# Attention outputs in the two column halves of the array, v rows with their neighbours, and an earlier begin of the first GEMM

## The chip, the cores and the metric

The kernel runs on one core of a Trainium2 chip. The metric is the device time of one execution in microseconds (us), lower is better. The runs of the kernel before took 255.43 us in the median of three (255.09 to 257.05). Differences of less than about 1% cannot be told from none.

The engines are TensorE (PE: matmuls into the accumulation memory, PSUM, and beside them weight loads, PEld), VectorE (DVE), ScalarE (ACT), GpSimd (POOL) and SyncE (SP). GpSimd and SyncE also issue DMAs. Each engine works through its own instructions in order and waits on semaphores of the others.

## What is computed

For 4 batches, 8 heads, 768 positions and head size 64, attention with a local window and block summaries, then a feed-forward layer with a hard-swish:

```python
k_sum = k.reshape(B, H, nb, 32, D).max(axis=3)       # nb = 24 blocks of 32 keys
v_sum = v.reshape(B, H, nb, 32, D).mean(axis=3)
scores_l = q k^T / sqrt(D), kept where |i - j| < 16
scores_s = q k_sum^T / sqrt(D) + log(32)
a = softmax([scores_l, scores_s])
x = a @ [v, v_sum]                                    # heads side by side: 3072 x 512
h = x @ w_in                                          # 512 x 2048
out = (h * clip(h + 3, 0, 6) / 6) @ w_out             # 2048 x 512
```

## The kernel before, in words

A query block has 64 positions. The keys that it can see are its own 64, the 16 before and the 16 after, and the 24 block summaries: 120 of 128 rows of a contraction. So for each head and query block one matmul makes the scores, transposed (keys on the rows, 64 queries on the columns), and one makes the values. The heads are handled in four pairs (head p with head p + 4); a batch has two halves of 384 positions, six query blocks each. One half of a batch is one tile of the feed-forward layer, so there are eight tiles of 384 rows.

The steps, by their helper and line in the kernel before:

- `load` (L220), `load_vf` (L237), `edges_v` (L262), `load_v` (L273), `load_vrows` (L280), `load_w_in`, `load_w_out`: loads, all issued on GpSimd's queue. At most eight of them are under way: the ninth is issued when the first has landed.
- `Tk`, `Tq` (L495, L537): transposes of k and q by TensorE, 96 rows at a time, head j of a pair into column half j; ScalarE and VectorE copy them out. `Tk` also makes the block maxima and copies each block's neighbours beside it (`side`, two copies).
- `Sc` (L566): scores `sp`, 12 matmuls per pair and half, head j in row half j of the array; exp on ScalarE (L588), the mask on VectorE (L591).
- `AV` (L602): values `nd`. For each head and query block a matmul of the 128 key rows with 128 weight columns, of which one half are v and the other half fill. For batches 0 and 1 the fill is zero: both heads accumulate into one PSUM tile `num` (L618), and two more matmuls with ones give the sums of the exponentials in `den` (L623). For batches 2 and 3 (`DEN_IN_VALUES`, L29) the fill is ones: one matmul gives values and denominator together, `num` and `den` hold one head each with the halves swapped, and the logarithm and the final multiply are done in two instructions of 64 rows (L631, L632, L644, L645) in place of one of 128 (L634, L647). L635 turns the logarithm into a reciprocal.
- `F1` (L662): GEMM 1 of a tile, 16 column blocks of four matmuls (one per pair) into `hp` (L672), a ReLU on ScalarE (L677) and a min-and-multiply on VectorE (L680) into `g`.
- `F2` (L688): GEMM 2, 48 matmuls of 512 columns per tile (L700), in groups of three; each finished block of 128 rows is copied by ScalarE (L705) and stored by SyncE (L707).

The key rows of v stand in two buffers, `va[0]` for even batches and `va[1]` for odd ones: rows 0 to 63 own keys, 64 to 87 block sums, 96 to 111 the next 16 keys, 112 to 127 the previous 16. For batches 1 to 3 one DMA per four heads loads the own rows (L275) and two per four heads the edges (L266); v is loaded once more as rows of 32 keys (L283), GpSimd adds them to block sums (`vsum`, L288, five additions per four heads), and SyncE spreads the sums to all query blocks, one put per pair and four heads (L298). SyncE's puts and its output stores stand in one queue, in order. Batch 0 does not wait for this: v is loaded in float32 (`vf`), cast by three engines (L254), and its sums come from TensorE (`sum_v`, L725) and are copied to the query blocks (L743).

The order of the instructions on each engine comes from a planner (`class Plan`, L33). Each operation is added with an engine, an estimated cost, keys that it reads and writes, the buffers that it takes and a place; the planner simulates the engines and emits, engine by engine, the ready operation with the lowest place. A place is a number on a scale where each GEMM column block is one step: negative places are the start-up, 0 to 15 is GEMM 1 of tile 0, and so on. `attention(b, s)` (L803) puts the attention of batch b into the GEMM slots before tile 2b. In idle time at the start the planner puts `fill` matmuls on TensorE (L429).

## Time and profile before

| | |
|---|---|
| median of three runs | 255.43 us |
| the profiled execution's own time | 252.96 us |
| its span, first to last instruction | 251.3 us |
| mean granted TensorE clock | 0.986 |
| GEMM 1: 512 matmuls of 384 columns | 94.3 us busy |
| GEMM 2: 384 matmuls of 512 columns (358 in the records) | 90.0 us busy |
| values: 384 matmuls of 64 columns, and 32 with ones of 384 | 17.1 and 8.2 us busy |
| moved by DMA | 28.33 MB in 53851 packets |

How to read it: a busy time of matmuls counts each from its start to the modelled end, so neighbours overlap; the pace is better read from the starts in the timeline. Rows of groups give line, engine, operation, output and input, shape and count, then the busy time and the mean of one in ns, then the idle time of the engine before them and what ended it. In the timeline a row is a run of equal instructions: start, time covered, engine, line. DMA rows end with the median time from issue to landing.

### The profile page before, as it was taken

The numbers are of one execution on the slowest core, as the hardware profiler recorded it, in microseconds if no ns is written. First come the engines' busy times: TensorE is split into PE (matmuls) and PEld (weight loads), VectorE is DVE, ScalarE is ACT, GpSimd is POOL, SyncE is SP. The second block draws the span as 40 slices with busy tenths as digits, with TensorE's granted clock in tenths as the row PEclk, the third lists the DMA queues.
The fourth block names the chain that finished last, engine by engine and source line by source line (L and its number), as shares of the span: only waits on it lengthen the run. The fifth ranks groups of instructions, "written<-read, shape, count | busy, mean of one in ns | idle before, by whom it ended". The sixth has DMA issues, their size and how long they took to land.

```text
span 251.3 us, 5636 instructions
## 1 busy us (share of the span) xinstructions
PE 230.8 (92%) x2247; PEld 127.8 (51%) x2273; DVE 157.8 (63%) x309; ACT 163.5 (65%) x321; POOL 97.8 (39%) x134
## 2 busy tenths in 40 slices
PE   5899699999993997999989999999999999999993
PEld 1385456555552455665545555555455455555541
DVE  5568888658871237999687798468674735444400
ACT  2346679765650558986789885798786956555420
POOL 8985962757997704769990010000000000000000
PEclk9999999999997799999999999999999999999999
DMA  5999999999989999419992101100111021011112
GB/s 64 214 202 177 207 203 206 213 254 173 187 168 186 199 215 205 144 26 194 191 122 68 42 3 44 42 34 11 44 42 42 3 83 43 3 43 43 42 44 83
DMA packets 53851, 28.33 MB, mean 113 GB/s; under 512 B 39808, under 2 KB 49280, under 8 KB 53248
## 3 DMA queue, kind: packets, MB, share of 16 engines
q0 software_dynamic: 42384, 20.68, 62.5%
q1 hardware_dynamic: 11440, 7.28, 10.3%
q8 instruction: 18, 0.29, 0.5%
q14 instruction: 9, 0.07, 0.1%
HBM read 35.06 MB, written 6.29 MB: 165 GB/s over the span
## 4 chain that ended last, share of the span: by engine, by line
PE 79%; ACT 6%; DVE 5%; DMA 5%; issue 2%; POOL 1%; SPq 0%; ACTq 0%; POOLq 0%
PE hp L672 31%; PE op L700 30%; PE nd L618 4%; DMA va<-vs 3%; PE sums L729 3%; PE sp L584 3%; PE tpq L549 2%; PE fill L429 2%; PE tpk L504 2%; DMA stg<-in_k_dram 2%; PE nd L623 2%; DVE at L591 1%; ACT at L588 1%; ACT lg L635 1%; DVE g L680 1%
## 5 line engine op out<-in xcount | busy, mean ns | idle before, releaser
L677 ACT ACTIVATE r<-hp,half_c 128x384 f32<-128x384 f32 x128 | 71.9, 580 | 35.7 <-PE hp L672 32.1
L672 PE MATMUL hp<-x,win 128*128 128x384 bf16 x512 | 94.3, 326 | 0.7 <-DVE g L680 0.5
L700 PE MATMUL op<-wout,g 128*128 128x512 bf16 x358 | 90.0, 385 | 2.6 <-issue 1.8
L680 DVE SCALAR_TENSOR_TENSOR g<-r,hp 128x384 bf16<-128x384 f32 x128 | 67.6, 550 | 30.9 <-ACT r L677 28.2
L672 PEld LDWEIGHTS <-win 128*128 128x128 bf16 x512 | 48.0, 98 | 35.6 <-issue 2.0
L700 PEld LDWEIGHTS <-g 128*128 128x128 bf16 x384 | 36.0, 99 | 38.1 <-issue 1.9
L588 ACT ACTIVATE at<-sp 128x384 bf16<-128x384 f32 x64 | 27.7, 486 | 6.0 <-PE sp L584 5.9
L295 POOL TENSOR_TENSOR vr<-vr 96x1024 f32<-96x1024 f32 (+3 forms) x24 | 30.0, 1252 | 1.4
L591 DVE TENSOR_TENSOR at<-at,mask 128x768 bf16<-128x768 bf16 x32 | 21.9, 683 | 9.0 <-ACT at L588 8.8
L618 PE MATMUL nd<-at,va 128*128 128x64 bf16 x384 | 17.1, 194 | 6.7 <-DMA va<-vs 3.7
L705 ACT COPY ot<-op 128x512 f32<-128x512 f32 x24 | 14.1, 587 | 12.8 <-PE op L700 12.8
L618 PEld LDWEIGHTS <-va 128*128 128x128 bf16 x384 | 15.2, 98 | 11.9 <-issue 7.8
L523 POOL COPY kx<-kx 128x176 bf16<-128x176 bf16 x8 | 2.7, 334 | 45.0 <-ACT kx L507 45.0
L515 DVE TENSOR_REDUCE red<-tpk 128x24 bf16<-128x768 bf16 x16 | 15.3, 953 | 6.5 <-ACT kx L507 6.2
L507 ACT COPY kx<-tpk 128x768 bf16<-128x768 bf16 x16 | 12.8, 800 | 7.7 <-PE tpk L504 7.7
L647 DVE TENSOR_TENSOR x<-nd,lg 128x384 bf16<-128x384 f32 x16 | 8.9, 556 | 14.1 <-ACT lg L635 14.0
L635 ACT ACTIVATE lg<-lg 128x384 f32<-128x384 f32 x32 | 16.7, 523 | 1.0
L644 DVE TENSOR_TENSOR x<-nd,lg 64x384 bf16<-64x384 f32 x16 | 8.8, 549 | 13.3 <-ACT lg L635 12.2
L634 ACT ACTIVATE lg<-nd 128x384 f32<-128x384 f32 x16 | 7.9, 494 | 13.4 <-PE nd L623 13.2
L555 DVE COPY qx<-tpq 128x768 bf16<-128x768 bf16 (+1 forms) x16 | 13.4, 849 | 2.0 <-PE tpq L549 1.9
L584 PEld LDWEIGHTS <-kx 64*128 64x128 bf16 x384 | 7.6, 96 | 12.4 <-issue 11.4
L266 POOL DMA_DIRECT2D va<-in_v_dram x16 | 11.4, 715 | 4.2 <-DMA va<-in_v_dram 2.1
(60 smaller groups left out, 182.8 us busy)
## 6 DMA issues: line engine op xcount, KB each, us to landing
out_dram<-ot SPq DMA_DIRECT2D x24, 256.0 KB
vr<-in_v_dram POOLq DMA_DIRECT2D x6, 768.0 KB, 12.8
stg<-in_q_dram POOLq DMA_DIRECT2D x7, 384.0 KB, 13.4
stg<-in_k_dram POOLq DMA_DIRECT2D x6, 384.0 KB, 13.6
va<-in_v_dram POOLq DMA_DIRECT2D x6, 384.0 KB, 12.6
wout<-in_moe_w_out_dram POOLq DMA_DIRECT2D x4, 512.0 KB, 18.0
vf<-in_v_dram POOLq DMA_DIRECT2D x4, 384.0 KB, 7.1
win<-in_moe_w_in_dram POOLq DMA_DIRECT2D x2, 768.0 KB, 12.4
```

The lines of the kernel that those rows point to most:

```text
L295: nc.gpsimd.tensor_tensor(out=o, in0=r[:, 0:n], in1=r[:, n:2 * n], op=ALU.add)
L515: nc.vector.tensor_reduce(red[0][:], tp[:].rearrange("p (s n c) -> p n s c", s=RUN, n=NB), axis=AX.XY, op=ALU.max)
L584: nc.tensor.matmul(sp[j][:, u], kx[rows, p, t], qx[rows, p, t * QB:(t + 1) * QB], start=not on_pe, stop=not on_pe or u == NH - 1)
L588: nc.scalar.activation(a[:, j], sp_t[keys[j]][:], AF.Exp, scale=scl)
L591: nc.vector.tensor_tensor(a, a, msk.unsqueeze(1).to_broadcast([128, 2, NH, QB]), op=ALU.mult)
L618: nc.tensor.matmul((num, den)[j * two][:, u * QB:(u + 1) * QB], w, a[:, j, t], start=two or (u == 0 and j == 0), stop=two or (u == NH - 1 ...
L635: nc.scalar.activation(lg[:], lg[:], AF.Exp, scale=-1.0)
L672: nc.tensor.matmul(hp[:], w_in_sb[:, kt, ft * 128:(ft + 1) * 128], xt[t][:, kt], start=(kt == 0), stop=(kt == NP - 1))
L677: nc.scalar.activation(r[:], c[0][:], AF.Relu, bias=half_c[:], scale=1.0 / 6.0)
L680: nc.vector.scalar_tensor_tensor(gt[t][:, ft], c[1][:], 1.0, c[0][:], op0=ALU.min, op1=ALU.mult)
L700: nc.tensor.matmul(ops[t, ts][:], gt[t][:, ft, ts * 128:(ts + 1) * 128], w_out_sb[:, ft], start=(ft == 0), stop=(ft == NFT - 1))
L705: nc.scalar.copy(o[:], ops[t, ts][:])
```

## The change

1. **Values in column halves.** `AV` no longer has fill columns. Head j's matmul has 64 weight columns (v alone) and writes rows 64 j to 64 j + 63 of `num`; the two heads alternate, query block by query block. Two matmuls with 64 columns of ones write `den` in the same way, now in all four batches. `DEN_IN_VALUES`, the fills (`between`) and the two-instruction forms of logarithm and multiply are gone.
2. **v rows with both neighbours adjacent.** A block's rows are now the previous 16, its own 64 and the next 16 (rows 0 to 95), then sums and padding (96 to 127). One DMA per four heads loads 96 overlapping rows for 46 of the 48 blocks of four heads, two small ones the first and last block of each group. For batch 0 v is loaded shifted by 16 rows, so the casts can take the neighbours out of the loaded tile; the four edge DMAs of batch 0 are gone, the last 16 rows come in a small tile `vz`. `side` is one copy in place of two, the mask is built for the new rows.
3. **Sums of batch 0, first half,** are added by two matmuls per pair (`vsz` as weights) in place of copies into `va[0]`; a further matmul per pair brings in the rows of `vz`.
4. **GEMM 1 of tile 0** is begun with three pairs: its first four column blocks run their first three matmuls before pair 3's x is there, and the fourth later.
5. **Places.** The places of nearly all start-up and attention steps are set by a table, the order of the start-up loads by a list; the mask comes after all pair loads; fills are of 256 columns.

The core of the diff:

```diff
+PLACES = {
+    "a1": [18, 17, 25, 29, 33, 51],
+    "a2": [61, 61, 61, 70, 70, 84],
+    "a3": [80, 79, 87, 84, 100, 110],
+    "st": [3.5, 3, 3.5],
+    "ld": [2, 42, 94],
+    "vs": [-8, -4, 6],
...
+    "sl": "k0 I k1 q0 v2 J v0 q1 k2 k3 q2 Z v1 q3 v3 M W0 H W1 O".split(),
...
-    va = [const.tile([128, NV, 3, D], BF16, tag=f"va{i}", name=f"va{i}") for i in range(2)]
-    vj = [t[:, :, 0:3:2].rearrange("r n j d -> r j n d") for t in va]
+    va = [const.tile([128, 2, NV, D], BF16, tag=f"va{i}", name=f"va{i}") for i in range(2)]
...
+    def rows_v(b, first, rows, step, n):
+        return bass.AP(v.tensor, v.offset + (b * H * S + first) * D, [(D, rows), (step * D, n), (1, D)])
...
     def load_v(b, j):
         def issue():
-            nc.gpsimd.dma_start(out=vj[b % 2][0:QB, j],
-                                in_=v[b, NP * j:NP * j + NP].rearrange("h (t r) d -> r (h t) d", r=QB))
+            nc.gpsimd.dma_start(out=va[b % 2][0:R_SUM, j, 1:NV - 1], in_=rows_v(b, j * NP * S + QB - EDGE, R_SUM, QB, NV - 2))
...
         def pe():
             num, den = [(ps_o if alt else ps_n).tile([128, HALF], F32, tag=tag, name="nd") for tag in tags]
+            for u in range(NH):
+                t = half * NH + u
+                for j in range(2):
+                    nc.tensor.matmul(num[64 * j:64 * j + 64, u * QB:(u + 1) * QB], va[i][:, j, NQ * p + t], a[:, j, t],
+                                     start=not add_sums or u == 0, stop=not add_sums)
+            if add_sums:
+                for j in range(2):
+                    nc.tensor.matmul(num[64 * j:64 * j + 64].rearrange("p (t c) -> p t c", c=QB), vsz[:, p, j],
+                                     a[:, j, half * NH:(half + 1) * NH], start=False, stop=True)
             for j in range(2):
-                for u in range(NH):
-                    t = half * NH + u
-                    w = va[i][:, NQ * p + t].rearrange("p j d -> p (j d)")[:, j * D:j * D + 128]
-                    nc.tensor.matmul((num, den)[j * two][:, u * QB:(u + 1) * QB], w, a[:, j, t],
-                                     start=two or (u == 0 and j == 0), stop=two or (u == NH - 1 and j == 1))
-            if not two:
-                w = ones[:].rearrange("p j d -> p (j d)")
-                for j in range(2):
-                    nc.tensor.matmul(den[:].rearrange("p (t c) -> p t c", c=QB), w[:, j * D:j * D + 128],
-                                     a[:, j, half * NH:(half + 1) * NH], start=(j == 0), stop=(j == 1))
+                nc.tensor.matmul(den[64 * j:64 * j + 64].rearrange("p (t c) -> p t c", c=QB), ones[:],
+                                 a[:, j, half * NH:(half + 1) * NH], start=True, stop=True)
...
-            if two:
-                nc.scalar.activation(lg[0:64], num[64:128], AF.Ln)
-                nc.scalar.activation(lg[64:128], den[0:64], AF.Ln)
-            else:
-                nc.scalar.activation(lg[:], den[:], AF.Ln)
+            nc.scalar.activation(lg[:], den[:], AF.Ln)
...
-            if two:
-                nc.vector.tensor_tensor(xt[s][0:64, p], num[0:64], lg[0:64], op=ALU.mult)
-                nc.vector.tensor_tensor(xt[s][64:128, p], den[64:128], lg[64:128], op=ALU.mult)
-            else:
-                nc.vector.tensor_tensor(xt[s][:, p], num[:], lg[:], op=ALU.mult)
+            nc.vector.tensor_tensor(xt[s][:, p], num[:], lg[:], op=ALU.mult)
...
+        early = t == 0 and ft < 4
...
+        if early:
+            at_place(-120 + ft)
+            op("PE", 0.49, pe_first, wi + both(f"x{t}", NP - 1), [key], takes, tail=0.1)
+            plan.uses(f"x{t}")
+            at_place(ft)
+            op("PE", 0.163, pe_last, [f"x{t}{NP - 1}"], [key], (), tail=0.1)
```

In the order that the planner then gives: pair 0's values of batch 0 stand before the block sums of pairs 2 and 3 on TensorE (before, all sums came first); the first values of batch 1 stand after the same number of GEMM 1 matmuls (128) and after 63 GEMM 2 matmuls (60 before). On SyncE the queue is: two stores, one put, a store, seven puts, three stores (before: two stores, four puts, a store, four puts).

More of the change, by code (lines that the diff above doesn't have):

```diff
@@ new lines @@
+    op("DVE", 0.4, c_ind, (), ["ind0"])
+    for n_th, c in enumerate(PLACES["sl"]):
+        at_place(-999 + 0.01 * n_th)
+        if c == "I":
+            op("POOL", 0.55, c_ident, (), ["ident"])
+        elif c == "M":
+            op("POOL", 2.2, c_mask, ["band"], ["maskb"])
+        elif c == "J":
+            op("POOL", 0.5, c_ind2, ["ind0"], ["ind"])
+        elif c == "Z":
+            load_vz()
+        elif c == "H":
+            load("q", 0, slice(0, H), "1", 1)
+        elif c[0] == "W":
+            load_w_in(int(c[1]))
+        elif c == "O":
+            for c in range(4):
+                load_w_out(c)
+        elif c[0] == "k":
+            load_pair("k", int(c[1]))
+        elif c[0] == "q":
+            load_pair("q", int(c[1]), 0)
+        elif c[0] == "v":
+            load_vf(int(c[1]))
@@ L434 @@
     for i in range(NFILL):
[L435 removed]
+        op("PE", 0.11, fill, ["idle"], [f"fill{i}"], (("den", f"fill{i}"),), tail=0.0)
         plan.ops[-1]["spare"] = True
```

333 lines of the change are left out of this document (172 added, 161 removed).

## The prediction

> **What bounds the kernel now.** I read the page first: engine shares, the granted clock by slice, the chain that ended last.
>
> ```profile
> span 251.3 us, 5636 instructions
> PE 230.8 (92%) x2247; PEld 127.8 (51%) x2273; DVE 157.8 (63%) x309; ACT 163.5 (65%) x321; POOL 97.8 (39%) x134
> ...
> PEclk9999999999997799999999999999999999999999
> ...
> PE 79%; ACT 6%; DVE 5%; DMA 5%; issue 2%; POOL 1%; SPq 0%; ACTq 0%; POOLq 0%
> ```
>
> TensorE carries 79% of the chain, so the question is how much of its 251.3 us is matmul at full pace and where the rest lies. Only one place has a lowered clock, slices 13 and 14. Next the busy time by stage, with bounds at the first GEMM 1 matmul (32.5), the first attention of batch 1 (75.9) and the first GEMM 1 of tile 2 (98.4):
>
> ```profile
> 32.48:75.90 43.42, 42.78 (x440) 23.96 (x445) 32.62 (x62) 30.33 (x59) 30.05 (x33) 1.00 1.41 202
> 75.90:86.40 10.50, 6.47 (x62) 3.13 (x62) 1.58 (x6) 2.56 (x6) 7.66 (x9) 0.67 1.82 182
> 86.40:98.38 11.98, 10.52 (x156) 5.86 (x154) 5.38 (x10) 9.16 (x20) 2.31 (x5) 1.00 1.40 211
> 98.38:200.00 101.62, 98.82 (x1053) 56.09 (x1065) 77.95 (x139) 82.47 (x168) 31.08 (x41) 1.00 0.42 70
> ```
>
> The columns are span, then busy PE, weight load, VectorE, ScalarE, GpSimd, then clock, DMA share, GB/s. From 32.5 to 75.9 TensorE is full. From 75.9 to 86.4 it is busy 6.5 of 10.5 us, and at a mean clock of 0.67. After 98.4 it is nearly full again. So the time that can be won lies before 32.5, in 75.9 to 98.4, and little elsewhere. In the first two stages the DMA engines are saturated (share above 1, about 200 GB/s): whatever is loaded there moves only if bytes or packets ahead of it go.
>
> Prices on TensorE at full clock, from starts in its timeline (a busy time includes the pipeline's tail, so the next start counts):
>
> ```profile
> 100.34 0.51 PE L618 MATMUL nd<-at,va 128*128 128x64 bf16 x12
> 100.69 0.49 PE L623 MATMUL nd<-at,ones 128*128 128x384 bf16 x2
> 101.11 0.35 PE L584 MATMUL sp<-qx,kx 64*128 64x64 bf16 x12
> 101.39 2.77 PE L672 MATMUL hp<-x,win 128*128 128x384 bf16 x16
> ...
> 107.11 0.53 PE L549 MATMUL tpq<-ident,stg 96*64 96x96 bf16 x16
> 107.57 0.82 PE L672 MATMUL hp<-x,win 128*128 128x384 bf16 x4
> 108.23 0.51 PE L618 MATMUL nd<-at,va 128*128 128x64 bf16 x12
> ...
> 108.90 0.81 PE L672 MATMUL hp<-x,win 128*128 128x384 bf16 x4
> ```
>
> Twelve value matmuls take 0.35 (29 ns each), the two ones matmuls 0.32 to 0.33 (108.23 to 108.90 is 0.67 for both kinds), or 0.42 when the row halves of the scores follow: a change of array shape costs about 0.09. Twelve score matmuls take 0.28 with the change back. Sixteen transposes, in column halves of 64 weight columns, take 0.46, change included. A GEMM 1 matmul takes 0.66 / 4 = 0.163, or 0.42 ns a column.
>
> **The change, part by part.**
>
> *Column halves.* Batches 0 and 1 had 12 + 2 full-width matmuls (0.67), batches 2 and 3 had 12 (0.35). Now each has 12 + 2 with 64 weight columns, the heads of a pair in the two halves of the array. No value matmul of that form is in the trace. Nearest are the transposes: 16 of 96 columns one after the other would be 16 x 96 x 0.42 ns = 0.65, and they take 0.46, so halves overlap. Upper end: the twelve at the transposes' mean (0.345), ones not overlapping (0.33), a change in and out (0.19): 0.87. Lower end: six pairs at 29 ns (0.17) plus one ones matmul (0.16), no changes: 0.34. I take 0.28 (the score row, also pairs of 64 columns, leaving included) + 0.16 + 0.09 entering = 0.53. After GEMM 1 starts there are 12 of the old long form (4 of batch 0, 8 of batch 1) and 16 of the short: 12 x (0.53 - 0.67) + 16 x (0.53 - 0.35) = **+1.2 us**, ends -4.0 and +10.7. So the array itself gains nothing; batches 2 and 3 pay for ones matmuls they did not have. The Trainium skill speaks against this part: "TensorEngine Tiling (Array Packing)", section Restrictions, says column tiling rules out fast weight load, and "TensorE: Matmul & The Clock Gate", section LDWEIGHTS, gives columns / 1.2 ns, an estimate of 53 ns for 64 columns. By that the twelve loads alone are 0.64 and this term would be about +14 instead of +1.2. The transposes disagree: they load 64 columns each and pass at 0.46 / 16 = 29 ns.
>
> *Extra work on TensorE in batch 0:* two matmuls per pair that add the block sums (4 x 0.16) and one more matmul per sum (4). They lie before GEMM 1, where TensorE waits for data; 0, and 1.1 if that cover is gone (sums at 0.114, from 2.7 us for 24).
>
> *ScalarE and VectorE in batches 2 and 3.*
>
> ```profile
> L647 DVE TENSOR_TENSOR x<-nd,lg 128x384 bf16<-128x384 f32 x16 | 8.9, 556 | 14.1 <-ACT lg L635 14.0
> ...
> L644 DVE TENSOR_TENSOR x<-nd,lg 64x384 bf16<-64x384 f32 x16 | 8.8, 549 | 13.3 <-ACT lg L635 12.2 <-PE sp L584 1.0
> ...
> L634 ACT ACTIVATE lg<-nd 128x384 f32<-128x384 f32 x16 | 7.9, 494 | 13.4 <-PE nd L623 13.2
> L631 ACT ACTIVATE lg<-nd 64x384 f32<-64x384 f32 x16 | 7.8, 487 | 2.2 <-PE nd L618 1.8
> ...
> L549 PEld LDWEIGHTS <-stg 96*64 96x64 bf16 x256 | 7.1, 112 | 6.0 <-issue 4.5 <-DMA stg<-in_q_dram 1.4
> ```
>
> Two half-height logarithms become one full one (2 x 0.49 to 0.49), two multiplies likewise (2 x 0.55 to 0.56): 7.7 us less ScalarE, 8.7 less VectorE. Neither is the bound: from 98.4 to 200 TensorE is idle 2.8 of 101.6 and, with short starts and restarts, loses some 5 us up to the end. The path from values to x is a microsecond shorter, and num/den come free sooner. I count **-1.5**, ends -3.5 and +2: every slot of the planner has moved, and a slot put too early stalls TensorE in order. The GpSimd fills between the heads go, rows for sums are cleared instead; GpSimd works 31 of 101.6 us there and bounds nothing.
>
> *Loading of v.* For batches 1 to 3 the packet count is the same: 64 x 48 x 2 + 4 x 16 x 47 = 9152 rows before, 96 x 46 x 2 + 2 x 80 x 2 = 9152 after; 0. For batch 0 the four edge DMAs (3008 rows) go; a load of 128 rows and one more split come in. The mask moves behind all pair loads on GpSimd's queue, where it delays weights by nothing: the queue waits for landings there.
>
> ```profile
> 14.04 2.90 POOL L266 DMA_DIRECT2D va<-in_v_dram x4
> ...
> 19.24 0.80 POOL L227 DMA_DIRECT2D stg<-in_q_dram  x1 [1.05 <-DMA vf<-in_v_dram]
> ...
> 21.91 0.62 ACT L254 CAST va<-vf 64x512 bf16<-64x512 f32 x1 [0.72 <-DMA vf<-in_v_dram]
> ...
> 30.66 0.53 PE L549 MATMUL tpq<-ident,stg 96*64 96x96 bf16 x16
> ```
>
> ```profile
> va<-in_v_dram POOLq DMA_DIRECT2D x4, 94.0 KB, 8.5
> ```
>
> ```profile
> stg<-in_q_dram POOLq DMA_DIRECT2D x1, 384.0 KB, 10.4
> ```
>
> The last v of batch 0 lands at 21.9. The edges, issued 14.0 to 16.9, land 8.5 later, so up to about 24.4: 2.5 us of a saturated queue, and their small packets also slow the v load beside them. Without them v should be in at about 20 and q's second half at 29.6 - 4 = 25.5 (it landed 19.2 + 10.4 = 29.6).
>
> *The start of GEMM 1.*
>
> ```profile
> 32.51 1.42 PE hp L672 x8
> ```
>
> Before, it started at 32.5 because sums of pairs 2 and 3 stood ahead of the first values, and x of all four pairs was needed. In the new order pair 0's values come before these sums, pair 2's x stands on VectorE behind two q copies (0.55 each), and 12 matmuls of three pairs cover pair 3's x. From q's landing at 25.5: two transposes and two copies 1.6, x 0.56, gives 27.7; I take 28.0, so **-4.5**. Ends: -6 (v and q limited by bytes alone) and -1.5 (three pairs save 0.9 and an edge DMA's 0.6, nothing else).
>
> *The wait at 75.9.*
>
> ```profile
> 75.93 0.34 PE L618 MATMUL nd<-at,va 128*128 128x64 bf16 x6
> 79.96 0.48 PE L618 MATMUL nd<-at,va 128*128 128x64 bf16 x6 [3.69 <-DMA va<-vs]
> ...
> 81.85 3.62 PE L700 MATMUL op<-wout,g 128*128 128x512 bf16 x8 [0.33 <-issue]
> 85.26 0.58 PE L618 MATMUL nd<-at,va 128*128 128x64 bf16 x12
> ...
> 86.38 2.76 PE L700 MATMUL op<-wout,g 128*128 128x512 bf16 x12
> 89.07 0.35 PE L584 MATMUL sp<-qx,kx 64*128 64x64 bf16 x12
> ```
>
> ```profile
> 71.55 0.34 SPq L707 DMA_DIRECT2D out_dram<-ot  x1
> 72.00 3.29 SPq L298 DMA_DIRECT2D va<-vs  x4
> ```
>
> ```profile
> 58.65 5.02 POOL L295 TENSOR_TENSOR vr<-vr 96x1024 f32<-96x1024 f32 x4
> ...
> 69.35 0.32 POOL L295 TENSOR_TENSOR vs<-vr 96x64 bf16<-96x64 f32 x1
> ```
>
> Values of the second head group wait for block sums of batch 1. GpSimd had them at 69.7, but SyncE issues in order and stood at the third output store until 71.55; the put went out at 72.0 and landed at about 79.9. After 3.7 us of idling the clock is halved: 9 GEMM 2 matmuls take 81.85 to 85.26, 3.4 us for 9 x 0.216 (2.69 less 0.09, over 12). From 75.93 to 86.38 pass 10.45 us for 3.9 of work: 6.5 lost. In the new order the third store stands ahead of seven of the eight puts again, but 15 GEMM 2 and 24 GEMM 1 matmuls and score work, about 8 us, follow it before the values, where there were 4.4 (71.55 to 75.93). TensorE arrives at 28.0 plus the stage's 43.4 and a little more work in front, 72. The sums, moved by the DMA queue's 2.5 to 3, are ready at 67, the store goes at about 65 (72 - 8 and its copy), the fifth put (the one needed) at 67.5, after four puts of 0.8; with 3 to 7 us to landing, 70.5 to 74.5. I leave 1.0 of the 6.5, too short to drop the clock: **-5.5**, ends 0 and -6.5. Late next is x of pair 3 of batch 1.
>
> *86.4 to 98.4:* 12.0 us hold 27 GEMM 2 matmuls (5.8) and 4.3 of attention, 1.9 lost on scores, logarithm and transposes before tile 2. The new order puts scores of both halves earlier; I leave 1.2: **-0.7**, ends -1.9 and +1.
>
> **Sum.** -4.5 + 1.2 - 5.5 - 0.7 - 1.5 = -11.0: span 240.3. The profiled execution took 252.96, 1.7 beyond its span, and would take 242. The median of the runs, 255.43, lies 2.5 above it; the same difference gives 255.4 - 11.0 = 244.4 for the median.
>
> **Rivals.**
> - *The wait for sums stays.* TensorE now arrives 4 us earlier, the sums only 3; if the put again needs 7.9 us to land (72.0 to 79.9) and the clock drops, 5.5 comes back: 250. Against: 8 us of work behind the store, not 4.4.
> - *The start is not won.* Pair 2's values wait on casts behind GpSimd's last weight issues, or q's half comes as late as before; GEMM 1 starts at 31: 247.5, or 249 if the wait at 72 suffers too.
> - *The halves do not overlap.* Then 0.87 each, +10.7 in place of +1.2: 254, no difference that shows.
> - *Slower: half-width weight loads are not hidden.* If each pair of value matmuls waits for one load of its length in the trace (112 ns, the weight-load row above), an attention step is 6 x 0.112 + 0.16 + 0.19 = 1.02, 0.49 more than I take, 28 times: +13.7, 258. It decides from 55 ns per matmul on. Against: the transposes pass at 29. The Trainium skill's 53 ns (above) would give 244.4 + 28 x 0.46, an estimate of 257.
>
> **Chances.** The forecast 0.66; the wait stays 0.13; the start not won 0.10; no overlap 0.06; slower 0.05. Runs of this kernel tell a difference from about 1% on (2.6 us): faster 0.88 (the first three), same 0.06, slower 0.06. The range leaves out the last two and the tail of good ends: 240 (the start at 26.5, the wait gone, the halves at 0.45) to 251 (wait kept and part of the start lost).
>
> **What would show it.** First GEMM 1 matmul at 26.5 to 29.5, with 12 matmuls of three pairs; no edge DMAs and v in by 20; no clock of 0.5 between 70 and 90 and values of batch 1 starting at 71 to 74; 12 + 2 half-width matmuls in 0.45 to 0.6; after tile 2's start a stretch as full as before. It is wrong if the halves take over 0.8, if a pause above 3 us stands anywhere after 30 us, or if ScalarE and not TensorE is the full engine after GEMM 1's start.

## The result, and the profile after

The changed kernel took 246.63 us in the median of four runs (245.38 to 247.06), the kernel before, on the same chip, 255.26 (253.37 to 257.05). The ratio is 0.966, 95% interval 0.958 to 0.973: faster by 3.4%. The forecast was 244.4, with 240 to 251 as its range. The profiled execution took 246.55, span 244.8; before's took 252.96, span 251.3, and lay 2.3 below its median. Between the two profiles, on which the steps below rest, the gain is therefore 6.5 us, where 11.0 were forecast. Runs more than 1.5% above the fastest of the same kernel are left out of all medians and ranges from here on; of the first kernel with the adds ahead, below, that leaves two times.

The page of the changed kernel, the same lines as were shown of before:

```profile
span 244.8 us, 5713 instructions
PE 234.0 (96%) x2331; PEld 123.4 (50%) x2331; DVE 149.1 (61%) x277; ACT 156.1 (64%) x305; POOL 91.9 (38%) x123
...
PEclk9999999999999799999999999999999999999999
...
PE 85%; DMA 5%; DVE 5%; ACT 2%; SPq 1%; issue 1%; POOL 1%; POOLq 0%
```

The chain that ended last is now 85% TensorE (79% before). One slice of lowered clock is left of two. The stages of the changed kernel, cut at its own first GEMM 1 matmul, first values of batch 1, second step of these values, and GEMM 1 of tile 2 (columns as in the prediction's table):

```profile
31.22:76.92 45.70, 44.32 (x475) 23.57 (x472) 36.22 (x64) 32.38 (x64) 31.96 (x37) 1.00 1.53 209
76.92:83.71 6.79, 4.43 (x36) 1.91 (x35) 1.47 (x3) 2.25 (x5) 0.00 (x0) 0.75 1.90 208
83.71:91.94 8.23, 8.23 (x120) 4.09 (x119) 2.99 (x6) 6.14 (x14) 0.00 (x0) 1.00 0.99 231
91.94:200.00 108.06, 108.06 (x1173) 56.70 (x1170) 72.62 (x130) 80.94 (x161) 32.02 (x36) 1.00 0.39 69
```

| stage | before | after | change | forecast |
|---|---|---|---|---|
| up to GEMM 1 | 32.5 | 31.2 | -1.3 | -4.5 |
| GEMM 1 to the first values of batch 1 | 43.4 | 45.7 | +2.3 | -0.6 |
| first values of batch 1 to GEMM 1 of tile 2 | 22.5 | 15.0 | -7.4 | -6.8 |
| GEMM 1 of tile 2 to the last matmul | 148.9 | 149.2 | +0.3 | +0.8 |
| behind the last matmul | 4.0 | 3.6 | -0.4 | 0 |

The forecast's +1.2 for the column halves is shared out here: -0.6 for each four of the long old steps (one in each of the three middle rows) and +2.9 for the 16 short ones, which stand in the fourth row with the -1.5 for ScalarE and VectorE.

The rows do not hold the same work before and after, as the order moved. The second holds three GEMM 2 and 24 score matmuls more now (1.2 us at the prediction's prices, 0.216 each and 0.28 a dozen). The third holds one step of values (five before, four now), twelve scores, three GEMM 2 and 32 transposes fewer, together 2.5 us. The step and the transposes stand in the fourth row now, which has twelve scores fewer: 1.3 us more. Like for like, an estimate from these prices, the three rows are +1.1, -4.9 and -1.0, where -0.6, -6.8 and +0.8 were forecast. (GEMM 2 of before is counted in its run with the stores moved, below, as some records of it are missing in the profile of before.)

After 91.9 TensorE is busy without a gap. Two things are out of line: the start, and the stage after it. TensorE's timeline at the start of the changed kernel:

```profile
17.69 2.77 PE L774 MATMUL sums<-vf,ind 128*32 128x128 f32 x12
20.39 0.63 PE L775 MATMUL sums<-vz,ind 32*32 32x128 f32 x2
20.95 1.62 PE L774 MATMUL sums<-vf,ind 128*32 128x128 f32 x12
...
24.14 1.50 PE L774 MATMUL sums<-vf,ind 128*32 128x128 f32 x12
25.57 0.40 PE L775 MATMUL sums<-vz,ind 32*32 32x128 f32 x2
25.90 0.38 PE L650 MATMUL nd<-at,va 128*64 128x64 bf16 x12
...
31.22 1.15 PE L700 MATMUL hp<-x,win 128*128 128x384 bf16 x6
```

From 17.7 to 31.2 no instruction waits: TensorE works through its order. A pair's block sums take 1.76 us from start to the next instruction at full clock (24.14 to 25.90), and 3.26 for the first pair (17.69 to 20.95), because the clock was still at half: the trace's first record of a full clock is at 21.2. Ahead of its first record the clock column of page and views reads full, so half clock is read there from the pace. And around the values of batch 1:

```profile
76.92 0.22 PE L650 MATMUL nd<-at,va 128*64 128x64 bf16 x1
79.49 0.53 PE L650 MATMUL nd<-at,va 128*64 128x64 bf16 x11 [2.36 <-DMA va<-vs]
...
80.71 3.07 PE L746 MATMUL op<-wout,g 128*128 128x512 bf16 x9
83.71 0.38 PE L650 MATMUL nd<-at,va 128*64 128x64 bf16 x12
```

SyncE's own queue at that time:

```profile
61.77 0.98 SPq L348 DMA_DIRECT2D va<-vs  x1
68.95 0.34 SPq L753 DMA_DIRECT2D out_dram<-ot  x1
69.34 7.87 SPq L348 DMA_DIRECT2D va<-vs  x7
```

The third output store went at 68.95, when ScalarE had made its copy; the seven puts stood behind it, the one that TensorE needed went out at 71.86 and landed 7.6 us later. The wait is 2.4 us instead of 3.7, but long enough for half a clock: nine GEMM 2 matmuls take 3.0 us (80.71 to 83.71), where nine take 1.95 at full speed.

### The profile page after: what moved, and what is told of

It is laid out like the page before. It is cut to its first block, busy times and chain, and to the rows that moved or that the text cites. A ratio compares the mean times of both kernels' runs of the same rounds, so it can differ in the third digit from the quotient of the medians.

```text
span 244.8 us, 5713 instructions
## 1 busy us (share of the span) xinstructions
PE 234.0 (96%) x2331; PEld 123.4 (50%) x2331; DVE 149.1 (61%) x277; ACT 156.1 (64%) x305; POOL 91.9 (38%) x123
## 4 chain that ended last, share of the span: by engine, by line
PE 85%; DMA 5%; DVE 5%; ACT 2%; SPq 1%; issue 1%; POOL 1%; POOLq 0%
PE op L746 32%; PE hp L700 32%; PE nd L650 4%; PE sp L616 3%; DMA va<-vs 3%; PE sums L774 3%; PE tpk L537 3%; PE fill L488 2%; PE tpq L581 2%; PE nd L657 2%; DMA stg<-in_k_dram 2%; DVE qx L587 1%; DVE kx L551 1%; DVE red L548 1%; SPq L348 1%; DVE g L717 1%
## 5 line engine op out<-in xcount | busy, mean ns | idle before, releaser
L700 PE MATMUL hp<-x,win 128*128 128x384 bf16 x512 | 95.8, 327 | 0.0
L746 PE MATMUL op<-wout,g 128*128 128x512 bf16 x384 | 95.3, 383 | 0.0
L717 DVE SCALAR_TENSOR_TENSOR g<-r,hp 128x384 bf16<-128x384 f32 x128 | 68.9, 551 | 40.6 <-ACT r L714 37.5
L620 ACT ACTIVATE at<-sp 128x384 bf16<-128x384 f32 x64 | 27.9, 488 | 8.9 <-PE sp L616 8.8
L345 POOL TENSOR_TENSOR vr<-vr 96x1024 f32<-96x1024 f32 (+3 forms) x24 | 29.5, 1230 | 8.7 <-DMA vr<-in_v_dram 7.2
L672 DVE TENSOR_TENSOR x<-nd,lg 128x384 bf16<-128x384 f32 x32 | 17.8, 556 | 20.7 <-ACT lg L664 20.6
L623 DVE TENSOR_TENSOR at<-at,mask 128x768 bf16<-128x768 bf16 x32 | 18.7, 588 | 9.4 <-ACT at L620 9.2
L663 ACT ACTIVATE lg<-nd 128x384 f32<-128x384 f32 x32 | 15.8, 492 | 11.5 <-PE nd L657 11.3
L557 POOL COPY kx<-kx 128x384 bf16<-128x384 bf16 x8 | 4.0, 508 | 32.6 <-ACT kx L540 32.6
L650 PEld LDWEIGHTS <-va 128*64 128x64 bf16 x384 | 8.9, 112 | 12.0 <-issue 8.6
L650 PE MATMUL nd<-at,va 128*64 128x64 bf16 x384 | 12.4, 200 | 2.4 <-DMA va<-vs 2.4
L616 PE MATMUL sp<-qx,kx 64*128 64x64 bf16 x384 | 11.8, 196 | 0.8 <-ACT at L620 0.8
## 6 DMA issues: line engine op xcount, KB each, us to landing
wout<-in_moe_w_out_dram POOLq DMA_DIRECT2D x4, 512.0 KB, 18.5
```

Source lines behind the costliest of these rows:

```text
L345: nc.gpsimd.tensor_tensor(out=o, in0=r[:, 0:n], in1=r[:, n:2 * n], op=ALU.add)
L616: nc.tensor.matmul(sp[j][:, u], kx[rows, p, t], qx[rows, p, t * QB:(t + 1) * QB], start=not on_pe, stop=not on_pe or u == NH - 1)
L620: nc.scalar.activation(a[:, j], sp_t[keys[j]][:], AF.Exp, scale=scl)
L623: nc.vector.tensor_tensor(a, a, msk.unsqueeze(1).to_broadcast([128, 2, NH, QB]), op=ALU.mult)
L650: nc.tensor.matmul(num[64 * j:64 * j + 64, u * QB:(u + 1) * QB], va[i][:, j, NQ * p + t], a[:, j, t], start=not add_sums or u == 0, stop=n ...
L672: nc.vector.tensor_tensor(xt[s][:, p], num[:], lg[:], op=ALU.mult)
```

## The experiments

All times are medians of up to four runs (ten for the last kernel) beside runs of the kernel before on the same chip. Those gave 254.08 for the first four kernels, 252.77 for the next four, 252.18 for the last four, so that differences under some 2 us between kernels of different groups rest on their traces.

**One sum matmul per pair (first group).** Five of the six matmuls over v rows are left out, so batch 0's block sums are wrong; order and waits stay.

```diff
-            for s in range(NT):
+            for s in range(NT - 1, NT):
-                ... start=(s == 0), stop=False)
+                ... start=True, stop=False)
```

> Batch 0's block sums on TensorE are cut from six matmuls per pair to one (and the small one), so the sums come out wrong; the order on every engine is that of the changed kernel. Theory: after v has landed, TensorE's own in-order work sets the start of GEMM 1; the four sums take 1.4 to 2.7 us each there, 7.1 us together (17.69 to 28.57), and cutting them takes about 6 us off. GEMM 1 then starts when q's second half and its copies allow, at 26.5 to 27.5 in place of 31.2, and the kernel takes 242 to 243.5. Rival: casts on VectorE and GpSimd, the masks and the logarithms set it; the start moves by less than 1.5 us, to 30 or later, and the kernel takes 245.5 or more.

Measured: 246.49 us (244.63 to 247.51), no difference to the changed kernel. GEMM 1 starts at 29.6, 1.6 earlier; 5 x 4 matmuls less at the changed kernel's 1.43 / 6 = 0.24 each would be 4.8. Much of the rest went into the clock:

```profile
20.73 0.53 PE L581 MATMUL tpq<-ident,stg 96*64 96x96 bf16 x8
21.06 0.52 PE L650 MATMUL nd<-at,va 128*64 128x64 bf16 x12
...
29.61 2.10 PE L700 MATMUL hp<-x,win 128*128 128x384 bf16 x6
...
31.94 1.31 PE L700 MATMUL hp<-x,win 128*128 128x384 bf16 x7
```

Six GEMM 1 matmuls take 2.0 us at 29.6 (1.08 in the changed kernel), and full speed comes at 31.7, not 21.2; that alone takes back 0.95 of the 1.6 us. All of it is gone at the first values of batch 1, which start at 77.0 as before. So the sums do stand in the way of the start, but beside the clock something between GEMM 1 and 77 takes the gain back.

**The halves one after the other (first group).** Six values of head 0, then six of head 1, in place of alternating.

```diff
-            for u in range(NH):
-                t = half * NH + u
-                for j in range(2):
+            for j in range(2):
+                for u in range(NH):
+                    t = half * NH + u
```

> The same value matmuls in the column halves, but all six of head j = 0 first and then all six of j = 1, so neighbours stand in the same half. Theory: the halves overlap only where neighbours alternate; the twelve go from 0.19 to 0.21 us to about 0.35, as twelve full-width ones, 32 times 0.15 is 4.8 us, of which those before GEMM 1 are partly hidden: 250 to 251.5. Rival: TensorE finds the other half's work by itself, or is bound by something else; 246 to 247.5.

Measured: 247.25 us (246.80 to 247.29). The step before a GEMM 1 block, in this kernel's timeline and then in the changed kernel's:

```profile
92.95 0.40 PE L650 MATMUL nd<-at,va 128*64 128x64 bf16 x10
...
93.51 0.82 PE L700 MATMUL hp<-x,win 128*128 128x384 bf16 x4
```

```profile
91.94 2.12 PE L700 MATMUL hp<-x,win 128*128 128x384 bf16 x12
93.99 0.38 PE L650 MATMUL nd<-at,va 128*64 128x64 bf16 x12
94.20 0.33 PE L657 MATMUL nd<-at,ones 128*64 128x384 bf16 x2
94.47 0.82 PE L700 MATMUL hp<-x,win 128*128 128x384 bf16 x4
```

Twelve values and two ones matmuls take 0.48 alternating (93.99 to 94.47) and 0.56 in turn (92.95 to 93.51). Twelve GEMM 1 matmuls ahead of a step take 2.05, 0.09 more than 12 x 0.163: the change of shape on the way in. A step so costs 0.57; forecast 0.53. Alternating is worth 0.08 a step, no more. In turn, too, the twelve keep well under the 0.35 of full-width ones.

The times hide a second difference. TensorE waited at the first values of batch 1 here too, almost as long, but the clock stayed full:

```profile
79.61 0.28 PE L650 MATMUL nd<-at,va 128*64 128x64 bf16 x3 [2.25 <-DMA va<-vs]
...
80.37 2.12 PE L746 MATMUL op<-wout,g 128*128 128x512 bf16 x9
```

So GEMM 1 of tile 2 starts 1.0 earlier than in the changed kernel (90.9), and the stretch from there to the end of the span is 1.7 longer, 0.08 for each of the 20 steps in it.

**Output stores on ScalarE's queue (first group)**, in the changed kernel and, as a second run, in the kernel before:

```diff
-            nc.sync.dma_start(out=out[row:row + 128], in_=o[:])
+            nc.scalar.dma_start(out=out[row:row + 128], in_=o[:])
```

> The output stores are issued from ScalarE's queue behind the copy that makes them; SyncE's queue then holds the puts of the block sums alone. All else stands in the same order. Theory: the puts of batch 1 stood behind the third store (68.95); now the fifth put goes when its sums are ready, at about 67.2 in place of 71.9, and with the same 7.6 us to landing is in at 74.8, before TensorE comes at 76.9: no wait of 2.4, no clock of 0.5, 3 to 4 us less: 242.5 to 244. Rival: the landing is set by the loads that share the DMA engines, which are the long ones of q and k until about 77.5; the put lands at 77 or later whenever it is issued, the wait stays over 0.5 us: 245 to 247. If issuing a store costs ScalarE much (24 stores), GEMM 1 slows down: over 247.

> The same move of the stores in the kernel before, nothing else. Theory: its wait at 75.9 to 80.0 came from the store at 71.55 that stood ahead of the second group of puts; they then go at about 69.7, 2.3 us earlier, land at 77 to 78, and 1.5 to 2.5 us of the wait and perhaps the halved clock (2.7 us more) go: 250 to 254. Rival: landing is set by the loads: 254.5 to 256.

Measured: 242.94 us (242.69 to 243.25) for the changed kernel so edited, ratio to before 0.955 (0.951 to 0.960); 249.49 (248.72 to 250.62) for the kernel before, 0.982 (0.976 to 0.987). SyncE and TensorE of the first:

```profile
61.88 8.66 SPq L348 DMA_DIRECT2D va<-vs  x8
```

```profile
77.03 0.38 PE L650 MATMUL nd<-at,va 128*64 128x64 bf16 x12
...
77.79 2.12 PE L746 MATMUL op<-wout,g 128*128 128x512 bf16 x9
```

All eight puts are out by 70.5, the wait is gone, the clock stays. TensorE arrives as before (77.03) and is at GEMM 1 of tile 2 at 88.1 in place of 91.9. In the kernel before, TensorE still waits 1.1 us for a put (3.7 without the edit), but the clock stays full, and 4.6 us are won, a little more than expected. So the wait came from SyncE's order, in both kernels, and in the changed kernel 3.9 us (91.94 to 88.06) were still to be had. The rival has a share: the put that TensorE needs goes out at 67.30, 4.6 earlier, but is under way for 9.3 us and lands at 76.6, 2.9 earlier and only 0.5 before TensorE comes. With the stores out of the way in both, the change is worth 6.5 us (249.49 to 242.94).

**Three pairs undone (second group).** GEMM 1 of tile 0 waits for all four pairs.

```diff
-        early = t == 0 and ft < 4
+        early = False
```

> The changed kernel with its first part undone alone: GEMM 1 of tile 0 waits for all four pairs again. Theory 1 (a gain at the start is eaten up before 77 us, since VectorE is full from 55 to 70 us and TensorE waits on it at 65): GEMM 1 starts about 0.5 us later than 31.2, the first values of batch 1 still start within 0.3 of 76.9, and the time stays within 0.4 of the changed kernel's 246.6. Theory 2 (what the start loses is lost for good): the first values of batch 1 and the time move with the start, 247.1 or more.

Measured: 244.81 us (244.58 to 245.06), ratio 0.969 (0.965 to 0.973): not slower than with three pairs. GEMM 1 starts at 33.3, 2.1 later, four times what was expected, and yet the first values of batch 1 start at 75.8, 1.1 earlier. Neither theory had that. But the planner moved more than the three pairs. Six GEMM 2 and twelve score matmuls, some 1.6 us, no longer stand in front of these values, and seven puts stand ahead of the third store:

```profile
64.67 6.15 SPq L348 DMA_DIRECT2D va<-vs  x7
73.52 0.34 SPq L753 DMA_DIRECT2D out_dram<-ot  x1
73.91 0.82 SPq L348 DMA_DIRECT2D va<-vs  x1
```

The wait for the puts is 0.6, and the clock keeps full speed: this kernel got by its order some of what the stores on ScalarE's queue gave. Beside that kernel, where the wait is gone, its span is 2.4 longer (243.3 against 240.9) and GEMM 1 of tile 2 starts 1.3 later (89.3 against 88.1). So the run does not show what the three pairs are worth by themselves.

**Small copies on ScalarE (second group)**, with the stores on ScalarE's queue. In the changed kernel VectorE is full from 55 to 65 (third pair of columns behind the span: 4.97 and 5.00 of 5 us):

```profile
55.00:60.00 5.00, 5.00 (x54) 2.63 (x53) 4.97 (x9) 3.31 (x6) 4.86 (x3) 1.00 2.20 184
60.00:65.00 5.00, 4.53 (x65) 2.44 (x63) 5.00 (x7) 1.38 (x3) 4.69 (x6) 1.00 1.96 190
```

Some of its copies stand out:

```profile
54.91 1.35 DVE L551 COPY kx<-red 128x288 bf16<-128x288 bf16 x1
...
58.20 0.54 DVE L551 COPY kx<-red 128x288 bf16<-128x288 bf16 x1
...
62.35 1.80 DVE L551 COPY kx<-red 128x288 bf16<-128x288 bf16 x1
...
68.69 0.22 DVE L551 COPY kx<-red 128x288 bf16<-128x288 bf16 x1
```

GpSimd issues a load and adds just then:

```profile
54.50 1.73 POOL L318 DMA_DIRECT2D va<-in_v_dram  x1 [3.03 <-ACT kx L540]
56.30 5.06 POOL L345 TENSOR_TENSOR vr<-vr 96x1024 f32<-96x1024 f32 x4
...
61.71 5.05 POOL L345 TENSOR_TENSOR vr<-vr 96x1024 f32<-96x1024 f32 x4
```

Each slow copy ends within 0.1 us of the end of one GpSimd instruction: the first (56.26) with the issue of the load (56.23), and not, as the expectation has it, with an add; the second and third (58.74, 64.15) with the first and longest add of a group (58.64, 64.06).

```diff
-            nc.vector.tensor_copy(kx[:, p, :, R_SUM:R_SUM + NB], ...)
+            copy = nc.scalar.copy if b == 1 else nc.vector.tensor_copy
+            copy(kx[:, p, :, R_SUM:R_SUM + NB], ...)
-        edges = nc.vector if b == 1 else nc.gpsimd
+        edges = nc.scalar if b == 1 else nc.gpsimd
```

> The kernel with its stores on ScalarE's queue (242.9), and the two small copies per pair that finish the keys of batch 1 made by ScalarE in place of VectorE. Theory 1 (these copies on VectorE stand still while an add of GpSimd runs: 1.35 and 1.80 us in place of 0.22, and VectorE, full from 55 to 70, hands that on to TensorE at 65): VectorE is below 4.6 of 5 us busy in 55 to 65, the wait of the key transposes at 65 goes, the first values of batch 1 start 0.5 to 1.5 us before 77.0 and the time is 241.5 to 242.4. Theory 2 (the arrival at 77 is set by TensorE's own work from 46 on): it stays at 77.0 within 0.2 and the time at 242.9 within 0.4. Were ScalarE held up by the same adds, its copies would show over 1 us.

Measured: 242.00 us (241.72 to 242.15). VectorE and TensorE in 55 to 65:

```profile
55.00:60.00 5.00, 5.00 (x55) 2.60 (x52) 4.42 (x7) 4.93 (x11) 4.69 (x3) 1.00 2.07 190
60.00:65.00 5.00, 5.00 (x83) 3.09 (x83) 3.87 (x6) 1.94 (x5) 4.69 (x6) 1.00 2.14 184
```

VectorE has room again, TensorE is full (4.53 of 5 in 60 to 65 in the changed kernel), the first values of batch 1 start at 76.0 in place of 77.0, and the same copy takes 0.44 on ScalarE, while GpSimd adds. Theory 1 stands by the trace, though the edit takes the copies themselves off VectorE together with their waits; of the 0.9 us in the times the two groups cannot be sure. The Trainium skill has this on the page "SBUF — State Buffer", section "Who interferes with whom": VectorE's copies in a two-port mode and a GpSimd instruction exclude each other for the whole instruction, and ScalarE waits for no one. The trace agrees in both: 0.22 against 1.80 on VectorE, 0.44 on ScalarE.

**Sums side by side (second group)**, with the two edits above: the block sums of two pairs in two column groups of 32, matmul by matmul in turn.

```diff
+                for n in ps:
+                    nc.tensor.matmul(sums[rows[n]], ind[...], vf_t[0][:, n:H:NP, s], ...)
```

> The one above, and the sums of two pairs made side by side in two column groups of TensorE's array (28 matmuls in two groups in place of 56 in one). Theory 1 (the sums stand ahead of the values in TensorE's order and cost the start some 1.5 us at 1.76 a pair; what is won there lasts once VectorE is clear): GEMM 1 starts 1 to 2 us before 31.2 and 0.7 or more of it is still there at the first values of batch 1, time 240.3 to 241.7. Theory 2 (the clock decides the start: less work, later full speed): the clock is at half until after 24 us, the start is won by less than 1 us, and the time is that of the kernel above within 0.4.

Measured: 244.23 us (242.95 to 246.49), 2 slower than without it. GEMM 1 starts at 29.4 and the first values of batch 1 at 73.3, 1.7 and 2.7 earlier. But of the 2.7 some 1.6 are six GEMM 2 and twelve score matmuls that stand behind these values in this order, so about 1.1 of the 1.7 last. There the puts are late again (1.1 us: the sums are in at 74.6) and GEMM 1 waits 1.3 for gating on VectorE; GEMM 1 of tile 2 starts at 87.4, 0.3 after the kernel without it. Neither theory: most of the gain lasts to 73 and is lost at the next waits.

**Idle matmuls in bursts (second group)**, with the stores on ScalarE's queue. The `fill` matmuls each wait for the one before, some 0.2 us. Here the first nine are three bursts of five, the others come in twos. (The changed kernel's nine take 3.81 us, the bursts' fifteen the same 3.81.)

```diff
+        n = (5 if i % 3 == 0 else 0) if i < 9 else 2
+        for _ in range(n):
             nc.tensor.matmul(t[:, 0:256], idle[:, 0:128], idle[:, 0:256], start=True, stop=True)
```

> The kernel with its stores on ScalarE's queue (242.9), with the idle matmuls ahead of the data in the same order and of the same total, but in bursts without gaps (three of five matmuls, then two at a time, where single ones left about 0.2 us between them). Theory 1 (the clock comes about 4 us after TensorE has no gaps; the single idle matmuls do not raise it): full clock from 7 to 14 us on in place of 21, and GEMM 1 starts 1 to 2 us before 31.2. Theory 2 (the clock comes at a fixed time, or with real work alone): full clock from 20 to 22 us as before, start at 31.2 within 0.4. The time by either theory is 242.0 to 243.3, since by VectorE's full stretch the start is lost again.

Measured: 240.70 us (239.29 to 240.76), ratio 0.951 (0.945 to 0.957), the fastest kernel of this study. Full clock comes at 5.0 in place of 21.2, by the first clock record and by the pace of the transposes (0.53 for sixteen, 0.85 in the changed kernel):

```profile
1.27 3.81 PE L491 MATMUL fill<-idle 128*128 128x256 bf16 x15 [1.27 <-DVE idle L484]
5.00 0.53 PE L540 MATMUL tpk<-ident,stg 96*64 96x96 bf16 x16
...
15.79 1.50 PE L777 MATMUL sums<-vf,ind 128*32 128x128 f32 x12
...
17.54 1.50 PE L777 MATMUL sums<-vf,ind 128*32 128x128 f32 x12
...
27.76 1.15 PE L703 MATMUL hp<-x,win 128*128 128x384 bf16 x6
```

The first pair's sums take 1.75 (15.79 to 17.54) where they took 3.26, and GEMM 1 starts at 27.8, the forecast's 28.0. Of the 3.6 us won on the kernel with the stores alone (31.4) 3.1 are left at the first values of batch 1 (73.9), against what both theories said of the time. There 0.9 goes on the puts, and the span is 2.0 below that of the kernel with the stores alone (240.9 to 238.9).

**Edge transfers put back (third group).** Four DMAs like those of before behind batch 0's v, to rows that are written again later.

```diff
+            if g == 3:
+                for j in range(2):
+                    src = v[0, NP * j:NP * j + NP].rearrange("h (t r) d -> r (h t) d", r=QB)
+                    for i, (rows, at) in enumerate(((slice(0, EDGE), 1), (slice(QB - EDGE, QB), 0))):
+                        nc.gpsimd.dma_start(out=va[1][EDGE * i:EDGE * i + EDGE, j, 0:NV - 1], in_=src[rows, at:at + NV - 1])
```

> The changed kernel with four transfers of 16-row edges, as the kernel before had them for batch 0, put back behind the last load of v (into rows of the second value tile that are written again later). Theory 1 (the transfers that went were worth nothing to the start, since in the changed kernel the second half of q landed at 24.2 and the start waits on TensorE's order until 31.2): the second half of q lands 2 to 3 us later, GEMM 1 still starts at 31.2 within 0.5, time 246.6 within 0.6. Theory 2 (the start follows the transfers): GEMM 1 starts at 32.5 or later and the time is 247.5 or more.

Measured: 247.81 us (247.09 to 249.78), ratio to before 0.985 (0.977 to 0.993), where the changed kernel had 0.966. The last v lands at 19.5 and q's second half at 27.0 (18.5 and 24.2 in the changed kernel); GEMM 1 starts at 32.4, 1.15 later, which is nearly theory 2; but 0.8 of it is there already in the second pair's sums, ahead of any use of q, where the clock also came 1.3 us later (22.6). The first values of batch 1 start 0.5 later, but the wait there grows to 3.8 us and the half clock lasts twice as long, so GEMM 1 of tile 2 starts at 95.2, 3.2 later. The profiled execution was the slowest of the four (249.78; the others took 247.97 or less). The transfers taken out were worth about one microsecond of the start; what they were worth in the time, 1.2 us by the medians and some 5 by the ratios, is not settled.

**The adds ahead (third group)**: stores, bursts and small copies as above, and GpSimd's adds for batch 1 ahead of its next load of v; then the same with the sums side by side; then the same with four pairs.

```diff
-        plan.add("POOL", 0.8, place(), issue, (), [f"va{b % 2}O{j}"], dma=4.4)
+        plan.add("POOL", 0.8, place(), issue, ["vr10"] if b == 2 else (), [f"va{b % 2}O{j}"], dma=4.4)
```

> Stores on ScalarE's queue, idle matmuls in bursts, the small copies of batch 1 on ScalarE, and GpSimd's adds for the sums of batch 1 ahead of its next load of v (in the kernel with bursts that load stood at 54.85 to 56.6 ahead of them, while the rows had landed at 54.0). Theory 1 (with the start won and VectorE cleared, the sums of batch 1 come last, 0.9 us too late there): the adds start near 54.5 and end 1.5 to 2 us before 67.5, the wait for the puts at the first values of batch 1 goes, and the time is 238.3 to 239.7 where bursts alone gave 240.7. Theory 2 (ScalarE and VectorE behind the values of batch 1 take back what is won, as with the sums side by side, 244.2): GEMM 1 waits for the gating by 1 us or more after the first values and the time is 240.5 to 242.5.

> The one above with the sums of batch 0 of two pairs side by side. Theory 1: GEMM 1 starts 1 us or more before 27.8, and 0.5 us or more of it is left in the time, 237.5 to 239. Theory 2 (its order brings the values of batch 1 too early for the transfers and engines behind them): the first values come before 73.5, the waits for puts, gating and masks that follow are over 1.5 us, and the time is that of the kernel above or up to 2 us more.

> The one before last, but GEMM 1 of tile 0 waits for all four pairs. Theory 1 (the three pairs pay, once what eats the gain is gone): 0.4 to 2 us slower than with three pairs. Theory 2 (they are worth nothing in any order, as in the changed kernel, 244.8 without them against 246.6): the same within 0.5, or faster.

Measured: 246.3 us (245.84 and 246.73), 247.51 (246.98 to 250.27), 249.45 (247.86 to 251.40), ratios to before 0.978, 0.985 and 0.992: all 5 us or more slower than the bursts with the stores. The adds did end earlier, at 64.8 in the second (67.5 with the bursts alone), but the puts behind them landed at 74.0 in place of 75.0, so most of the 2.7 us was lost in the transfer. Two things went wrong. The planner's later order moved with the edit: from GEMM 1 of tile 2 to that of tile 7 pass 124.5 and 124.7 us in the last two, where the changed kernel and all others made from it have 120.3 to 122.3. TensorE now waits for VectorE's gating there, as theory 2 had it in kind but not in size, in the second at 120.8 and at 138.7:

```profile
120.77 0.81 PE L704 MATMUL hp<-x,win 128*128 128x384 bf16 x4 [2.12 <-DVE g L721]
```

And the bursts did not always hold the clock, which no theory had. In the second kernel it was full from 6.4 on and GEMM 1 started at 27.9; in the third it was full from 5.5 to 8.9, TensorE stood for 1.8 us of these on a late load of keys, and it was at half until 22.6 and GEMM 1 at 35.8. These three say nothing, then, on whether three pairs pay.

## Why the prediction was right, and where it was wrong

*Direction and size* came out: 246.6 against 244.4. Part of that is luck. The profile of before lay lower than its median; by the profiles the forecast was 4.5 us too good. And the terms missed on both sides: the start and the wait, the two largest, gave 6.2 less than forecast, the stretch up to tile 2 and the relief behind it more. The signs that were named for these two did not show: GEMM 1 started at 31.2 and not by 29.5, the values of batch 1 at 76.9 and not by 74, and a clock of 0.5 stood between 70 and 90.

*The start of GEMM 1* is the step that failed: -1.3 in place of -4.5, beyond the poor end of -1.5. Its data part was right and even cautious: the last v landed at 18.5 (20 forecast), q's second half at 24.2 (25.5). Wrong was "before GEMM 1, where TensorE waits for data; 0, and 1.1 if that cover is gone". The cover was gone: from 17.7 TensorE had no gap, and four sums of 1.76 to 3.26 us, priced at 0.114 a matmul where a matmul of this shape takes 1.43 / 6 = 0.24, stood between it and the values. The price was read off records that show each such matmul twice. Beside it stands the half clock up to 21.2: the kernel with bursts has the same sums, the same data and full clock, and starts at 27.8. Fewer sums won 1.6, with the clock at half until 31.7; full clock with all sums won 3.6, which is what was missing.

*From GEMM 1 to batch 1* 43.4 "and a little more" became 45.7, forecast as a stage that moves unchanged. Of the 2.3 us 1.5 are TensorE's busy time, 1.2 of them the three GEMM 2 and 24 score matmuls more, and 0.7 idle. The trace with the small copies on ScalarE gives 0.8 of it to VectorE behind GpSimd's adds. This stretch also takes back part of what the start wins or loses: four kernels that began GEMM 1 between 29.6 and 31.4 all arrived at 76.9 to 77.0, and of the 1.15 us lost with the edge transfers 0.5 were left there. How much it takes back differs: with the bursts 3.1 of 3.6 us lasted. (The kernel that began at 33.3 and arrived at 75.8 had 1.6 us less work in front.) That the full VectorE is the reason is not shown. This stays open.

*The wait at batch 1* was forecast as -5.5. By the prediction's own account, 6.5 were lost there before; after, 76.92 to 84.47 is 7.55 for 3.5 of work, 4.0 lost: -2.5. The store "at about 65" went at 68.95, the put from 67.5 at 71.86, and it took 7.6 to land, beyond "3 to 7". This was the first rival, half true: arrival came later than 72, too, so 2.4 us of wait were left. The stores taken out of SyncE's queue show directly that the late store held the put back.

*The stretch up to tile 2* gave more than the forecast -0.7. Like for like the third row is -4.9; with -2.5 for the wait and -0.4 for its four steps (0.57 - 0.67 each) about -2 is left, near the good end. From 83.7 to 91.9 TensorE has no idle time. The prediction did not see that one of five steps and 32 transposes would move behind tile 2's start, so the row of -7.4 is no measure of it.

*Column halves*: 0.57 measured, 0.53 forecast. Both rivals about them fell: twelve values pass in 0.21 (93.99 to 94.20), a pair with its two weight loads in 35 ns, as the transposes had said; the loads of 112 ns each that the slower rival feared are in the trace and are hidden. Of the Trainium skill's rule on fast weight load under column tiling, named in the prediction, no cost is seen here. Batches 2 and 3 pay about as forecast, 16 x (0.57 - 0.35) = +3.5 for +2.9.

*The relief of ScalarE and VectorE* was sized too small. Behind tile 2's start 20 steps of 0.57 stand where 16 of 0.35 and three of 0.67 stood, with 32 transposes more (0.92) and twelve scores less (0.28): some 4.4 us more work, an estimate from these prices. The stage grew by 0.3, so the time lost there shrank by about 4.1, where 1.5 were forecast and 3.5 was the good end.

*The small packets of the edges* were priced at 2.5 us of queue: put back, they delayed q's half by 2.8, and the start by 1.15.

Two sums of the prediction are off by little: the first three chances add up to 0.89, not 0.88, and the good end of the column halves is -4.1, not -4.0.

## What to carry to other kernels

Before a gain in arriving data is counted, lay out the consuming engine's order from that moment on, at the clock that it then has: here the data came early and TensorE was not ready. A queue that issues in order hides a late store in front of an urgent transfer; look at it first, and give the two separate queues. Work moved to an earlier point is worth something only if the next engine in line is not full; follow it to the next wait before counting it, and expect a planner's later order to move with any edit: count the work in front of a point before comparing when two kernels reach it.

## What the hardware showed that was not expected

- The clock changes on a grid of 3.41 us: in the changed kernel it was full for 58.03 (17 times that) and then half for 3.41, in the kernel before half for 6.83. The Trainium skill's page "TensorE: Matmul & The Clock Gate", section "What's actually happening", gives a free-running window of 3413 ns, and the traces agree. Waits of 2.3 to 2.7 us cost one such window at half clock, waits of 3.7 and 3.8 cost two, waits of 0.9 and 1.1 none. Length alone does not decide: the wait of 2.25 with the halves in turn cost none. Counted on from the first clock record (20.1 there), an edge of the grid at 78.13 cuts that wait (77.36 to 79.61), and no window holds more than 1.5 us of it. In the second kernel with the adds ahead (first record 6.4, edges at 71.22 and 74.64) a wait of 2.28 lies in one window, and the clock is lost at its end; so it is with 2.14 of the 2.36 us in the changed kernel (edges at 75.86 and 79.27). Later in that second kernel a wait of 2.12 is cut at 119.01, has 1.76 in one window, and costs nothing.
- What a window must hold is not settled. The last kernel's TensorE, with the clock in the third column from the end:

```profile
8.50:12.00 3.50, 3.33 (x31) 1.60 (x30) 1.39 (x4) 1.18 (x3) 3.44 (x5) 0.56 1.14 198
12.00:15.50 3.50, 3.27 (x19) 1.45 (x18) 2.47 (x6) 1.63 (x4) 3.07 (x8) 0.50 1.22 236
15.50:19.00 3.50, 3.39 (x38) 1.71 (x38) 0.05 (x1) 1.36 (x3) 3.47 (x7) 0.50 0.95 161
```

  It is 3.3 of 3.5 us busy for over 10 us, by modelled ends, and stays at half. Single idle matmuls raised the clock in no kernel (it came between 16.5 and 31.7, with the real work), bursts in three of four, at 5.0 to 6.4, and once it was lost again, after a window with a wait of 1.8 us. In the fourth, the first with the adds ahead, the clock came at 23.8, with the real work; there an edge of the grid, at 3.3, cuts the bursts (1.27 to 5.08). That this is why is not shown.
- The put that TensorE waits for took 7.6 us from issue to landing while the DMA engines were full with large loads, 9.3 with the stores on ScalarE's queue. Making its sums 2.7 us earlier brought it 1.0 earlier.
